# Layer 1 on fewer slots than layer 2, in a mixture-of-experts stage behind linear attention

## The chip, the core and the metric

The kernel runs on one core of a Trainium2 chip. The metric is device time in microseconds (us), from the start to the end of one execution; the span of a profile is the time from its first to its last instruction. TensorE (PE in the profile, PEld for its weight loads) multiplies matrices, VectorE (DVE) and ScalarE (ACT) work on elements, GpSimd (POOL) issues the indirect DMAs here, and SyncE (SP) issues the loads of inputs and weights.

## The reference

```python
kv  = einsum('bhsd,bhse->bhde', k, v)          # 8 batches, 8 heads, 576 tokens, 64 wide
out = einsum('bhsd,bhde->bhse', q, kv)
out = out / sqrt(mean(out*out, -1) + 1e-6) * g_norm
x   = out as 4608 rows of 512
do_compute = x @ w_skip > 0                    # other rows leave as they are
e      = argmax(x @ w_gate)                    # one of 8 experts
gate_w = softmax(x @ w_gate)[e]
x[rows of e] += gate_w * (relu(x[rows of e] @ w1[e]) @ w2[e])   # w1 512x1024, w2 1024x512
```

With the inputs that the reference makes (its seed is fixed), 2265 of the 4608 rows go to an expert, in descending order of the counts 339, 333, 318, 275, 270, 264, 255 and 211.

## The kernel before, in words

**Attention** (up to about 128 us) goes through batches and units of tokens on all engines, writes the rows x to the output in DRAM, and ranks each row within its expert. Each expert has 384 numbered slots; the experts are put in descending order of their counts, and place r of that order has a fixed number of slots `CAPS[r]`: 352, 352, 320, 288, 288, 288, 256, 256. The table `srow` holds for each slot the row that stands in it (less 4608), from a memset to zero (L290) and two sums (`settle`, L706). `slot_rows` (L715) makes of it the row to scatter to; for an empty slot that is 4608, which is out of bounds, so that the scatter leaves it out (L1196). If an expert has more rows than slots, `rounds` (L1266) finds it and a loop (L1336) makes another round; the comparison is "more than".

**Experts.** A place's slots are cut into pieces (`plan_of`, L919): 128, 128 and then 64 or 32 rows (`kinds`, L258; `CAPS` must be sums of these). In `experts` (L1214), for r = 0 to 7 in this order: the weights of r+1 are issued on SP; where r is 7, GpSimd is drained (L1219); the rows of r+1 are gathered by GpSimd, one indirect DMA a piece (`gather_piece`, L940); layer 1 of r; the gathered rows of r+1 are transposed on TensorE (`expert_in`, L947; the first piece inside layer 1's last step, the rest behind it); layer 2 of r; and as each piece of layer 2 is done, VectorE scales and adds it and GpSimd scatters it (`result`, L1184).

For r = 0, layer 1 is plain matmuls over all slots but the first 128, which are done earlier. For r = 1 to 7, `fast_1` (L1064) makes layer 1 from seven products in place of eight, with the slots in two halves of `n = end // 2` columns: 7 products x 4 x 2 matmuls of n columns. `end` is the room of the pieces. A float32 matmul is two instructions in the profile, so a place has 112 of them. `fast_2` (L1124) does the same for layer 2 on the first 256 slots, in products of 256 columns, and does the pieces beyond as plain matmuls beside it. Every engine works in the order in which the code is written.

The hidden activations lie in a tile `ht` of 384 slots, two buffers; the rows of a place in `xg`, three buffers. A gather reads the output in DRAM, and so it waits for the landing of all scatters issued before it; GpSimd's queue holds, from the end of one place to the next, the scatters of r-1, then the gathers of r+1, then the scatters of r. At the program's end all engines go through a barrier (L1336, L1380), in which GpSimd is drained again.

Of the kernel before, what the change touches and what calls it, by code (L numbers as in the profile page):

```python
# [8 lines left out]
FP32 = mybir.dt.float32  # L9
# [3 lines left out]
ALU = mybir.AluOpType  # L13
# [4 lines left out]
def kernel(  # L18
# [43 lines left out]
    nc = tc.nc  # L62
# [3 lines left out]
    P = 128  # L66
# [6 lines left out]
    E, F = moe_w1.shape[0], moe_w1.shape[2]  # L73
# [4 lines left out]
    CAP = 384  # L78
    PK = 2 * KD

    KVD = 5
    CAPS = (352, 352, 320, 288, 288, 288, 256, 256)
    CK = CAP // 128
    NCOL = E * CK
    ROUNDS = N // CAP
    RSPACE = 8192
# [10 lines left out]
    setup = attn.enter_context(tc.tile_pool(name="setup", bufs=1))  # L97
# [114 lines left out]
    for a in range(2):  # L212
        r = slice(a * 64, (a + 1) * 64)
        nc.vector.tensor_scalar(out=gw_b[r, :, a, :, :],
                                in0=wraw[r, :, :].rearrange("e n (u w) -> e u w n", u=2),
# [15 lines left out]
    caps = keep.tile([P, E], FP32)  # L231
    for r, cap in enumerate(CAPS):
        nc.vector.memset(caps[:, r:r + 1], float(cap))

    number_f = keep.tile([P, CK], FP32)
# [8 lines left out]
    for i, qs in enumerate((slice(0, 4 * NQ), slice(4 * NQ, FQ))):  # L244
# [5 lines left out]
                                   op=ALU.bitwise_and)  # L250
# [3 lines left out]
                            in1=rest_i[:, :, :, :].rearrange("p f t r -> p (f t r)"), op=ALU.subtract)  # L254
# [1 line left out]


    kinds = {}  # L258
    for r, cap in enumerate(CAPS):
        off = cap // P * P  # L260
        for m in (64, 32):
            if cap - off >= m:
                kinds.setdefault((off % P, m), []).append((r, off))
                off += m
        assert off == cap
    again, part_of = {}, {}
    for lo, m in kinds:
# [5 lines left out]
        if m not in part_of:  # L273
            q_i = setup.tile([P, 1], I32, name=f"q_i{m}")
            nc.vector.tensor_single_scalar(out=q_i[:, :], in_=part_i[:, :],
                                           scalar=m.bit_length() - 1, op=ALU.arith_shift_right)
            q_f = keep.tile([P, 1], FP32, name=f"q_f{m}")
            nc.vector.tensor_single_scalar(out=q_f[:, :], in_=q_i[:, :], scalar=float(N * P // m),
                                           op=ALU.add)
# [7 lines left out]
    gate_k = keep.tile([P, NT, 3], BF16)  # L287

    srow = keep.tile([P, NCOL], FP32)
    nc.vector.memset(srow[:, :], 0.0)  # L290

    top = keep.tile([P, E], FP32)
    nc.vector.tensor_copy(out=top[:, :], in_=ebase[:, :])
# [336 lines left out]
    def drain(pieces):  # L630
        for _ in pieces:
            pass
# [134 lines left out]
    for b in range(KNOWN // S // 4 * 4, KNOWN // S):  # L767
        nc.gpsimd.dma_start(
            out=out[b * S:(b + 1) * S, :].rearrange("(p c) d -> p c d", c=C)[:, C - 1, :],
            in_=zero[:, :])  # L770

    todo = {}
# [74 lines left out]
    with tc.tile_pool(name="wpool_b", bufs=1, reuse_waits="tile") as wpool_b, \  # L847
# [6 lines left out]
        def bank():  # L854
            return ps_b.tile([P, 512], FP32, tag="bank", name="bank")
# [61 lines left out]


        def plan_of(r):  # L919
            pieces = [(c * P, P, r * CK + c) for c in range(CAPS[r] // P)]  # L920
            i = 0
            for (_, m), rs in kinds.items():
                for j, (r_, off) in enumerate(rs):
                    if r_ == r:
                        pieces.append((off, m, i + j))
                i += len(rs)
            return pieces

        plan = [plan_of(r) for r in range(E)]
        whole = [[(c * P, P, r * CK + c) for c in range(CK)] for r in range(E)]  # L930

        def x_of(xg, off, m):

            lo = (off % P) * DM // P if m < P else 0
            return xg[:, off // P, lo:lo + DM * m // P]
# [11 lines left out]
        def expert_in(xg, xt, piece):  # L947
            off, m, _ = piece
            x = x_of(xg, off, m)
            n = DC * m // P  # L950
            xp = bank()[:, :].rearrange("p (j t) -> p j t", t=P)
            for j in range(n):
                nc.tensor.transpose(out=xp[:, j, :], in_=x[:, j * P:(j + 1) * P],  # L953
                                    identity=ident[:, :])
            if m == P:
                nc.scalar.copy(out=xt[:, :, off:off + P], in_=xp[:, :, :])  # L956
            else:
                nc.scalar.copy(
                    out=xt[:, :, off:off + m].rearrange("p (q j) t -> p q j t", j=n),
                    in_=xp[:, 0:n, :].rearrange("p j (q t) -> p q j t", t=m))  # L960

        def new_xt():
            return ffn.tile([P, DC, CAP], FP32, tag="xt", name="xt")

        def new_ht():
            return ffn.tile([P, FC, CAP], FP32, tag="ht", name="ht")

        def layer_1(r, xt, ht, cols, fs):
            for f in fs:
# [241 lines left out]
                for piece in pieces[r]:  # L1211
                    gather_piece(xgs[r], piece, src, asrc)

        def experts(pieces, srcs, xt, ht, yps0, tables, group):  # L1214

            for r in range(E):
                load_ahead(r)
                if yps0 is not None and r == E - 1:
                    nc.gpsimd.drain()  # L1219
                if r:  # L1220
                    gather_all(r + 1, pieces, *srcs)
                todo = pieces[r]
                end = todo[-1][0] + todo[-1][1]
                new = {}

                def enter(some):
                    for piece in some:
                        expert_in(xgs[r + 1], new["xt"], piece)

                more = pieces[r + 1] if r + 1 < E else []  # L1230
                if more:
                    new["xt"] = new_xt()
                beside = []
                if r == 0:
                    if yps0 is not None:
                        tables = first_tables(lambda fs: layer_1(r, xt, ht, slice(P, end), fs), tables)
                        result((0, P, 0), yps0, xgs[0], tables, group)
                    else:
                        layer_1(r, xt, ht, slice(0, end), range(FC))
                    do(w1_sums(r + 1))  # L1240
                    enter(more)
                else:
                    fast_1(r, xt, ht, end // 2, w2_sums(r), lambda: enter(more[0:1]))
                    enter(more[1:])
                if more:
                    n = (more[-1][0] + more[-1][1]) // 2
                    beside = x_sums(r + 1, new["xt"], n) + (w1_sums(r + 1) if r else [])
                if r == 0:
                    for piece in todo:
                        result(piece, layer_2(r, ht, piece), xgs[r], tables, group)  # L1250
                        do(beside, 4)
                    do(beside)
                else:
                    if yps0 is not None and r == 1:
                        rnd_i = rounds()
                    if yps0 is not None and r == E - 1:
                        n_rounds.append(nc.values_load(rnd_i[0:1, 0:1], min_val=1,
                                                       max_val=ROUNDS + 1))
                    of = {piece[0:2]: piece for piece in todo}
                    fast_2(r, ht, todo[2:], beside,  # L1260
                           lambda key, y: result(of[key], y, xgs[r], tables, group))
                del w_sb[r]
                if more:
                    xt, ht = new["xt"], new_ht()

        def rounds():  # L1266

# [23 lines left out]
        first = (0, P, 0)  # L1291
        assert plan[0][0] == first
        plan[0] = plan[0][1:]
        xt0, ht0 = new_xt(), new_ht()
        expert_in(xg0, xt0, first)
        drain(choose(LAST))
        bv = columns(0, NE, colid_i, row_k, 2, gat_pool, NE)
# [6 lines left out]
        yps0 = layer_2(0, ht0, first, None, range(0, 3))  # L1304
        settle(NE, NT, last_bv)
        layer_2(0, ht0, first, yps0, range(3, 5))
        rows, src = slot_rows(slice(0, NCOL), slot_pool, "")
        arows, asrc = again_rows()
# [8 lines left out]
        def first_tables(layer, tables):  # L1317
# [8 lines left out]
            agate = slot_pool.tile([P, NRES], FP32, tag="agate", name="agate")  # L1326
            nc.vector.tensor_copy(out=agate[:, :], in_=again_of(gate))
            return (tables[0], gate), (tables[1], agate)
        experts(plan, (src, asrc), xt0, ht0, yps0, (rows, arows), "first")

        order.__exit__(None, None, None)

# [3 lines left out]
        with tc.For_i(1, n_rounds, 1):  # L1336
            nc.vector.tensor_single_scalar(out=colid[:, :], in_=colid[:, :], scalar=CK, op=ALU.add)
            nc.vector.tensor_single_scalar(out=number_f[:, :], in_=number_f[:, :],
                                           scalar=float(CAP), op=ALU.add)
            nc.vector.memset(srow[:, :], 0.0)  # L1340
            add_pieces(srow[:, :], place_all(colid, row_k, 2), 2)

            left = slot_pool.tile([P, NCOL], FP32, tag="left", name="left")
            nc.vector.tensor_tensor(
                out=left[:, :].rearrange("p (r c) -> p r c", c=CK),
                in0=number_f[:, :].unsqueeze(1).to_broadcast([P, E, CK]),
                in1=caps[:, :].unsqueeze(2).to_broadcast([P, E, CK]), op=ALU.is_ge)
            nc.vector.tensor_tensor(out=srow[:, :], in0=srow[:, :], in1=left[:, :], op=ALU.mult)
            rows, src = slot_rows(slice(0, NCOL), slot_pool, "")
            for r in range(2):  # L1350
                gather_all(r, whole, src, None)
            gate = slot_gates(colid)
            xt0 = new_xt()
            for piece in whole[0]:
                expert_in(xg0, xt0, piece)
            experts(whole, (src, None), xt0, new_ht(), None, ((rows, gate), None), "more")


# [26 lines left out]
```

## Time and profile before

| what | us |
|---|---|
| three runs | 404.02, 401.65, 402.52 (median 402.52) |
| the profiled execution's own time | 404.02 |
| its span, first to last instruction | 402.2 |
| mean granted TensorE clock | 0.956 of full |
| TensorE busy | 371.8 |
| VectorE busy | 254.4 |
| ScalarE busy | 144.7 |
| GpSimd busy | 123.5 |
| DMA | 81.70 MB at 203 GB/s |

The first 128 us of the span are attention, 128 to 182 the end of the ranking and place 0, then come places 1 to 7: place 1 from 182 to 219, places 2 to 6 in some 27 to 33 us each, place 7 from 369 to 394. The last scatter is issued at 395.5, and the rest is its landing and the end's barrier. A busy time is that of an engine's instructions; those of its queue (waits, branches, drains; written with a q, as POOLq) do not count in it. In a timeline, a line gives the start, the length, and in brackets how long the engine stood idle before and what ended that.

### The profile page before, as it was taken

To read this page: it belongs to the slowest core of one execution; us is meant where nothing else is said; L and a number is where in the kernel's file an instruction comes from. 1 tells how busy PE (TensorE), PEld (TensorE's weight loads), DVE (VectorE), ACT (ScalarE), POOL (GpSimd) and SP (SyncE) were. 2 spreads that over 40 slices of the span, in tenths; PEclk is the share of its full clock that TensorE was granted. 3 is DMA by queue.
4 is the path that set the end of the run, shared out by engine and by line. 5 is a ranking of instruction groups with operands and counts; after the bars stand their busy time and mean duration, and the time that the engine had idled before them with its cause. 6 is when DMAs were issued, how large, how long until landed. Compare 5 with 4: busy or idle time off the path is not lost.

```text
span 402.2 us, 9616 instructions
## 1 busy us (share of the span) xinstructions
PE 371.8 (92%) x3849; PEld 323.1 (80%) x3849; DVE 254.4 (63%) x621; ACT 144.7 (36%) x384; POOL 123.5 (31%) x192
## 2 busy tenths in 40 slices
PE   7789999999874989999999999999999999999992
PEld 4678988888763948859978987998988988989981
DVE  2233568899976761366674775766766776868811
ACT  1365786676743212203510440430430430431410
POOL 7024577665658243111204301231221111212001
PEclk9599999999986898999999999999999999999997
DMA  8999999898595882346252651752752752711001
GB/s 299 394 391 392 316 391 400 250 364 222 169 406 134 255 322 73 102 161 224 73 203 67 250 193 55 260 182 94 257 188 90 258 177 96 255 55 38 16 2 49
DMA packets 31287, 81.70 MB, mean 203 GB/s; under 512 B 1850, under 2 KB 1858, under 8 KB 31236
## 3 DMA queue, kind: packets, MB, share of 16 engines
q1 hardware_dynamic: 26688, 66.59, 47.9%
q0 software_dynamic: 4528, 14.41, 11.0%
q8 instruction: 32, 0.52, 0.5%
q14 instruction: 19, 0.16, 0.1%
q10 hardware_dynamic: 20, 0.02, 0.0%
HBM read 66.80 MB, written 14.48 MB: 202 GB/s over the span
## 4 chain that ended last, share of the span: by engine, by line
PE 71%; DVE 10%; issue 8%; ACT 4%; DMA 3%; POOL 2%; ACTq 0%; DVEq 0%; POOLq 0%
PE bank L1051 40%; PE bank L983 8%; PE bank L972 6%; PE o_ps L450 4%; DVE xl L489 3%; PE sum_ps L343 3%; PE q_ps L414 3%; PE bank L953 2%; DMA xg<-out_dram,src 2%; DVE rs L472 1%; PE g_ps L357 1%; DMA xb<-in_g_norm_dram 1%; ACT qT L417 1%; PE g_ps L366 1%; ACT rs L479 1%
## 5 line engine op out<-in xcount | busy, mean ns | idle before, releaser
L1061 ACT COPY p<-bank 128x144 f32<-128x144 f32 (+4 forms) x70 | 20.9, 299 | 106.1 <-PE bank L1051 91.9
L1051 PE MATMUL bank<-xt,w 128*128 128x144 f32 (+3 forms) x336 | 56.5, 291 | 0.0
L1051 PEld LDWEIGHTS bank<-xt,w 128*128 128x128 f32 x336 | 47.8, 190 | 1.9 <-DVE bank L1055 1.2
L1055 DVE TENSOR_TENSOR bank<-bank,p 128x144 f32<-128x144 f32 (+4 forms) x70 | 23.8, 340 | 40.3 <-PE bank L1051 38.5
L450 PE MATMUL o_ps<-kvd,qT 128*128 128x146 f32 x240 | 36.9, 296 | 3.8 <-DVE xl L489 1.4
L1193 POOL DMA_INDIRECT out_dram<-xg,rows x16 | 16.2, 1011 | 77.8 <-DVE xg L1190 77.2
L524 POOL TENSOR_TENSOR xb<-xl,g_b 128x512 f32<-128x512 f32 x32 | 38.2, 1193 | 1.2 <-DMA out_dram<-xb 1.2
L1051 PE MATMUL bank<-xs,s 128*128 128x144 f32 (+3 forms) x224 | 37.4, 292 | 0.0
L450 PEld LDWEIGHTS o_ps<-kvd,qT 128*128 128x128 f32 x240 | 32.5, 193 | 5.7 <-DVE xl L489 2.4
L983 PE MATMUL bank<-w,ht 128*32 128x128 f32 (+2 forms) x448 | 36.6, 322 | 0.0
L943 POOL DMA_INDIRECT xg<-out_dram,src x15 | 15.9, 1057 | 56.3 <-PE bank L1051 36.2
L1193 POOL DMA_INDIRECT out_dram<-xg,arows x8 | 9.0, 1129 | 76.9 <-DVE xg L1190 76.6
L1051 PEld LDWEIGHTS bank<-xs,s 128*128 128x128 f32 x224 | 31.6, 190 | 1.0 <-ACT p L1061 0.3
L472 DVE TENSOR_REDUCE rs<-sq 128x8 f32<-128x512 f32 x36 | 24.4, 679 | 12.3 <-ACT sq L464 12.1
L983 PEld LDWEIGHTS bank<-w,ht 128*32 128x32 f32 (+2 forms) x448 | 20.4, 121 | 13.6 <-issue 10.9
L489 DVE TENSOR_TENSOR xl<-o_ps,rs 128x584 f32<-128x584 f32 x33 | 25.3, 767 | 4.4 <-PE g_ps L366 0.5
L1051 PE MATMUL bank<-w,ht 128*128 128x256 f32 x112 | 27.2, 386 | 0.0
L1051 PE MATMUL bank<-t,ht 128*128 128x256 f32 x112 | 27.1, 385 | 0.0
L343 PE MATMUL sum_ps<-v,k 64*64 64x64 f32 x1152 | 25.3, 229 | 1.4 <-issue 0.9
L972 PE MATMUL bank<-xt,w 128*128 128x128 f32 (+1 forms) x128 | 24.4, 360 | 1.5 <-ACT xt L956 1.0
L343 PEld LDWEIGHTS sum_ps<-v,k 64*64 64x64 f32 x1152 | 21.7, 140 | 4.5 <-issue 2.6
L1051 PE MATMUL bank<-t,hs 128*128 128x256 f32 x112 | 25.3, 379 | 0.0
(198 smaller groups left out, 697.0 us busy)
## 6 DMA issues: line engine op xcount, KB each, us to landing
w<-in_moe_w_dram SPq DMA_DIRECT2D x16, 2048.0 KB, 10.3
q<-in_q_dram SPq DMA_DIRECT2D x8, 1152.0 KB, 12.0
k<-in_k_dram SPq DMA_DIRECT2D x7, 1152.0 KB, 12.2
v<-in_v_dram SPq DMA_DIRECT2D x7, 1152.0 KB, 14.7
out_dram<-xb SPq DMA_DIRECT2D x8, 512.0 KB, 8.1
out_dram<-xb POOLq DMA_DIRECT2D x8, 512.0 KB, 7.5
k<-in_k_dram SPq DMA_DIRECT2D x2, 576.0 KB, 4.8
v<-in_v_dram SPq DMA_DIRECT2D x2, 576.0 KB, 6.8
```

Of the source, the lines that this page charges most:

```text
L343: nc.tensor.matmul(out=sum_ps[w * 64:(w + 1) * 64, a, u, :], lhsT=kt[r, 2 * u + w, c, :], rhs=vt[r, 2 * u + w, c, :], start=(c == 0), stop ...
L450: nc.tensor.matmul(out=ps[:, w, 0:2 * PK].rearrange("p (r k) -> p r k", r=2)[:, :, cols], lhsT=qT[:, w, a, :], rhs=kvds[b % KVD][:, u, w, ...
L472: nc.vector.tensor_reduce(out=rs[:, :, :], in_=sq[:, :, :, :].rearrange("p x y (a d) -> p x (y a) d", a=2), axis=AX.X, op=ALU.add)
L489: nc.vector.tensor_tensor(out=xl[:, :, :, :].rearrange("p x y (a k) -> p x (y a) k", a=2), in0=ps[:, :, 0:2 * PK].rearrange("p x (h k) -> ...
L524: late.append(lambda: nc.gpsimd.tensor_tensor(out=xb[:, :, 4 * u * D:(4 * u + 4) * D].rearrange("p r (w x) -> p r w x", w=2), in0=xl[:, :, ...
L943: nc.gpsimd.indirect_dma_start(out=x_of(xg, off, m), out_offset=None, in_=cut_rows(m)[:, :], in_offset=bass.IndirectOffsetOnAxis(ap=idx[:, ...
L972: nc.tensor.matmul(out=hps[:, cols], lhsT=w_sb[r][0][:, dc, f * P:(f + 1) * P], rhs=xt[:, dc, cols], start=(dc == 0), stop=(dc == DC - 1))
L983: nc.tensor.matmul(out=yps[q * m:(q + 1) * m, 0:n], lhsT=ht[:, f, off:off + m], rhs=w_sb[r][1][:, f, q * n:(q + 1) * n], start=(f == 0), s ...
L1051: nc.tensor.matmul(out=out, lhsT=lhsT(i), rhs=rhs(i), start=start and i == 0, stop=i == k - 1, skip_group_check=True)
L1055: nc.vector.tensor_tensor(out=to, in0=x, in1=y, op=ALU.add)
L1061: nc.scalar.copy(out=t, in_=x)
L1193: ins = nc.gpsimd.indirect_dma_start(out=cut_rows(m)[:, :], out_offset=bass.IndirectOffsetOnAxis(ap=rows[:, col:col + 1], axis=0), in_=x, ...
```

## The change

The slots that layer 1 works on are parted from the room that is gathered, transposed and used by layer 2. `CAPS` becomes 344, 336, 320, 280, 272, 264, 256, 256, and `ROOMS` is each of them rounded up to a multiple of 32: 352, 352, 320, 288, 288, 288, 256, 256, the former `CAPS`. Pieces, gathers, transposes and layer 2 go by `ROOMS`. Layer 1 goes by `CAPS`: n in `fast_1` is 168, 160, 140, 136, 132, 128, 128 for r = 1 to 7 in place of 176, 160, 144, 144, 144, 128, 128; the plain matmuls of r = 0 have 216 columns in place of 224. GpSimd sets the part of `ht` between the two to zero (`blank`), once for r = 0 before the first transposes and for each later r at the end of the turn before. `srow` starts at 8192 for slots at and beyond `CAPS` and at zero for the others, by three VectorE operations in the setup in place of one memset, so that such a slot is never scattered. The drain of GpSimd at the start of the last place is gone.

```diff
-    CAPS = (352, 352, 320, 288, 288, 288, 256, 256)
+    CAPS = (344, 336, 320, 280, 272, 264, 256, 256)
+    ROOMS = tuple(-(-cap // 32) * 32 for cap in CAPS)
...
-    nc.vector.memset(srow[:, :], 0.0)
+    beyond = setup.tile([P, CK], FP32)
+    nc.vector.tensor_single_scalar(out=beyond[:, :], in_=number_f[:, :], scalar=float(CAP), op=ALU.add)
+    nc.vector.tensor_tensor(
+        out=srow[:, :].rearrange("p (r c) -> p r c", c=CK),
+        in0=beyond[:, :].unsqueeze(1).to_broadcast([P, E, CK]),
+        in1=caps[:, :].unsqueeze(2).to_broadcast([P, E, CK]), op=ALU.is_ge)
+    nc.vector.tensor_single_scalar(out=srow[:, :], in_=srow[:, :], scalar=float(RSPACE), op=ALU.mult)
...
+        def blank(ht, r):
+            if CAPS[r] < ROOMS[r]:
+                nc.gpsimd.memset(ht[:, :, CAPS[r]:ROOMS[r]], 0.0)
...
-        def experts(pieces, srcs, xt, ht, yps0, tables, group):
+        def experts(pieces, widths, srcs, xt, ht, yps0, tables, group):
...
-                if yps0 is not None and r == E - 1:
-                    nc.gpsimd.drain()
...
-                end = todo[-1][0] + todo[-1][1]
+                end = widths[r]
...
-                    n = (more[-1][0] + more[-1][1]) // 2
+                    n = widths[r + 1] // 2
...
                     xt, ht = new["xt"], new_ht()
+                    if yps0 is not None:
+                        blank(ht, r + 1)
...
         xt0, ht0 = new_xt(), new_ht()
+        blank(ht0, 0)
...
-        experts(plan, (src, asrc), xt0, ht0, yps0, (rows, arows), "first")
+        experts(plan, CAPS, (src, asrc), xt0, ht0, yps0, (rows, arows), "first")
```

In `kinds` and `plan_of`, `CAPS` is replaced by `ROOMS`; the loop for further rounds passes `(CAP,) * E` as widths.

More of the change, by code (lines that the diff above doesn't have):

```diff
@@ L258 @@
     kinds = {}
-    for r, cap in enumerate(CAPS):
+    for r, cap in enumerate(ROOMS):
         off = cap // P * P
@@ L919, in plan_of @@
         def plan_of(r):
-            pieces = [(c * P, P, r * CK + c) for c in range(CAPS[r] // P)]
+            pieces = [(c * P, P, r * CK + c) for c in range(ROOMS[r] // P)]
             i = 0
@@ L1355 @@
                 expert_in(xg0, xt0, piece)
-            experts(whole, (src, None), xt0, new_ht(), None, ((rows, gate), None), "more")
+            experts(whole, (CAP,) * E, (src, None), xt0, new_ht(), None, ((rows, gate), None), "more")
 _INS = ['q', 'k', 'v', 'g_norm', 'moe_w_skip', 'moe_w_gate', 'moe_w1', 'moe_w2']
```

## The prediction

> **What bounds the kernel now.** I read the page first: busy times, the chain that ended last, then TensorE by stretches.
>
> ```profile
> PE 371.8 (92%) x3849; PEld 323.1 (80%) x3849; DVE 254.4 (63%) x621; ACT 144.7 (36%) x384; POOL 123.5 (31%) x192
> PE 71%; DVE 10%; issue 8%; ACT 4%; DMA 3%; POOL 2%; ACTq 0%; DVEq 0%; POOLq 0%
> PE bank L1051 40%; PE bank L983 8%; PE bank L972 6%; PE o_ps L450 4%; DVE xl L489 3%; PE sum_ps L343 3%; PE q_ps L414 3%; PE bank L953 2%; DMA xg<-out_dram,src 2%; DVE rs L472 1%; PE g_ps L357 1%; DMA xb<-in_g_norm_dram 1%; ACT qT L417 1%; PE g_ps L366 1%; ACT rs L479 1%
> ```
>
> TensorE is the bound, the products of L1051 above all. But 2% of the chain is a DMA, the gather of the next place's rows, so a second limit is close. The table by stretches gives TensorE's busy time in the second column: place 1 fills its 37.00 us; places 3 to 5 leave 0.06, 0.08 and 0.18 of 30 free; place 6 leaves 0.71. The next view, the chain of waits at the end of layer 1 of place 4 (start, length, what), shows what these are.
>
> ```profile
> 296.12 0.49 PE bank L1051 x4
> 296.61 0.55 PE bank L953 x4
> 297.17 0.07 issue
> 297.23 0.30 PE bank L953
> ```
>
> The transposes of the next place's third piece (the second L953) begin only when its gather has landed: TensorE waits already. GpSimd's timeline has the reason (start, length, idle time before):
>
> ```profile
> 283.11 0.98 POOL L1193 DMA_INDIRECT out_dram<-xg,rows  x1 [0.30 <-DVE xg L1190]
> 291.44 0.99 POOL L943 DMA_INDIRECT xg<-out_dram,src  x1 [7.35 <-PE bank L1051]
> 292.74 0.97 POOL L943 DMA_INDIRECT xg<-out_dram,src  x1 [0.30 <-issue]
> 294.01 1.13 POOL L943 DMA_INDIRECT xg<-out_dram,asrc  x1 [0.30 <-issue]
> ```
>
> The last scatter is issued by 284.09, the first gather at 291.44. The view names TensorE for the 7.35 us between, but that work was long done: scatters take 7.3 us to land in the median, and a gather waits for the landing. Three gathers and some 3 us of landing follow. This row of DMAs starts when place 3's layer 2 ends, and layer 1's length does not enter it.
>
> **Layer 1's columns.** What a column costs is the spacing of equal matmuls in TensorE's timeline (start, length, ..., count):
>
> ```profile
> 185.38 0.76 PE L1051 MATMUL bank<-xt,s 128*128 128x176 f32 x4
> ...
> 196.72 0.76 PE L1051 MATMUL bank<-xt,s 128*128 128x176 f32 x4
> ...
> 284.49 0.65 PE L1051 MATMUL bank<-xt,s 128*128 128x144 f32 x4
> ...
> 293.80 0.65 PE L1051 MATMUL bank<-xt,s 128*128 128x144 f32 x4
> ...
> 343.88 0.61 PE L1051 MATMUL bank<-xs,s 128*128 128x128 f32 x4
> ...
> 352.38 0.61 PE L1051 MATMUL bank<-xs,w 128*128 128x128 f32 x4
> ```
>
> Between the starts of each pair lie 19 groups of four: (196.72 - 185.38)/76 = 149.2 ns at 176 columns, 122.5 ns at 144, 111.8 ns at 128. So a column is 0.83 ns from 144 to 176, and 0.67 from 128 to 144.
>
> - Place 0: 64 matmuls of 8 columns less. The first eight run at half clock (they take 3.4 us to the next groups' 1.5, after TensorE stood idle): (56 x 8 + 8 x 16) x 0.83 = **0.48 us**. All of it counts: VectorE's second table is ready at 161.94 and is used at 166.36, and all behind it waits for TensorE.
> - Place 1: 176 to 168, 112 x 8 x 0.83 = 0.74, taken as **0.73 us**. Its gathers land by 196.9, the last transposes start near 199.7; so 2 us of slack cover it.
> - Place 2: unchanged.
> - Places 3, 4, 5: 4, 8 and 12 columns at 0.67 x 112 are 0.30, 0.60 and 0.90, **1.8 us** in sum. I count them at **nothing**: TensorE waits for the gather here, and arriving earlier it waits longer. Bounds: 0 and -1.8 (all of it, if the gathers came earlier too).
> - Places 6, 7: unchanged.
>
> **The setup.** Three VectorE operations of 24 elements or fewer replace a memset that stands right ahead of work that TensorE waits for (L316, in the chain of waits):
>
> ```profile
> 11.55 0.08 DVE L290 MEMSET srow<- 128x24 f32 x1
> 11.74 0.55 DVE L316 MEMSET kvd<- 64x584 f32 x1
> 13.16 1.94 PE L357 MATMUL g_ps<-ident,kvd 128*128 128x64 f32 x8 [1.70 <-DVE kvd L316]
> ```
>
> Like operations elsewhere (L719, L722) take 0.18 and follow each other at 0.22. Three at 0.20 less the memset's 0.19 are **+0.4 us**; bounds 0 (taken up in attention, where VectorE and DMA also hold TensorE) and 0.6.
>
> **The blanks.** Five memsets of at most 192 elements a partition. The nearest row, 584 elements, is 5.01/8 = 0.63 us. They stand on GpSimd's queue behind the scatters of a place and ahead of the gathers, in the 7 us shown above (for place 0 in 11.4 us of idling before 144.81). What is queued behind them waits anyway, and layer 2 reads the blanks over 10 us later: **nothing**. If that cover were gone, 0.2 us each. Scatters and their bytes stay the same, since empty slots were out of bounds before as well.
>
> **The drain.** Its lines in the views of L1219 and L1380 (count: shortest/median/longest in ns, first and last start):
>
> ```profile
> L1219 POOLq DRAIN  x1: 6041/6041/6041, 369.9 to 369.9; - x1
> ...
> L1380 POOLq DRAIN  x3: 51/109/220, 401.2 to 402.0; - x3
> ```
>
> The drain that goes took 6.04 us, where GpSimd had nothing to do until 394.25: its going wins nothing there. Of it, 1.31 us is waiting for the scatter still being issued (to 371.24); 4.73 follow. That scatter's data had landed by 372.98, so for 3.0 us the drain was busy with something else. The first drain in the end's barrier took 0.220, behind two scatters; a drain at the program's start, with no DMA before, took 0.193. So its length depends on what lies before it. Two readings: (i) it works off something left by each DMA that GpSimd issued since the last drain: 57 before L1219 (23 gathers, 22 scatters, 12 of attention), 4.73/57 = 0.083 each, and two at the end would be 0.17, near the 0.220 seen; (ii) a fixed time has to pass from the last issue: the end's drain starts at 401.19, 4.67 us after its last scatter's 396.52, so that time was nearly over. By (i) the end's drain becomes some 59 x 0.083 = 4.9 us, **+4.7 us** on the path, as GpSimd is the last engine into that barrier and the others wait for it. By (ii) it stays 0.2. Bounds: 0 and 5.8 (all 6.04 less 0.22). I take (i), as it also says why the drain with two DMAs is hardly over the one with none; (ii) needs the end's drain to fall by chance just where the time runs out.
>
> The Trainium skill (VectorE: DVE Perf Modes, "The DRAIN you can't avoid") speaks against (i): it says that the drains of a kernel's beginning and end are a constant of about 12 ns on all five engines. In this trace that holds for the other four at the end (7 to 17 ns), not for GpSimd's, at 51 to 220 and 6041. By that rule the end would not lengthen, and the sum would be some 0.8 us below before.
>
> **The sum.** -0.48 - 0.73 + 0 + 0.4 + 4.7 = **+3.9 us**. Against the profiled execution (span 402.2, own time 404.02) that is a span of 406.1 and 407.9; that execution is 1.5 above the median of the three, and from the median, 402.52, it is **406.4 us**.
>
> **Rivals.**
> - *The end's drain stays short* (reading (ii)). Place: the barrier at 401.19. Then -0.48 - 0.73 + 0.4 = -0.8: **401.7 us**, not slower. It decides as soon as the drain costs under 2.8 us at the end (2.0 over before plus 0.8 won). For it: (ii) fits the one drain at the end; against it: the 0.193 and 0.220 side by side.
> - *Drain short, and the gathers come earlier as well*: -0.8 - 1.8 = -2.6, **399.9 us**. For it: landings vary with the weights' loads, which move too. Against it: the scatters' 7.3 us and the gathers' issue do not shorten.
> - *Drain long, gathers earlier*: +4.7 - 2.6 = +2.1, **404.6 us**.
> - *The change does not do what it says*: a place has more rows than slots, and a further round runs. The reference's counts against the slots, in order: 339/344, 333/336, 318/320, 275/280, 270/272, 264/264, 255/256, 211/256. All fit, the sixth exactly, and the test is "more than". Another round loads 16 weights of 10.3 us again: above **565 us**.
>
> **How the numbers follow.** A measurement here can tell some 0.5% (2.0 us) from no change. Chances: the forecast 0.55; short drain 0.26; short drain and earlier gathers 0.06; long drain and earlier gathers 0.07; a drain between 1 and 3 us 0.05; another round 0.01. The likeliest is 406.4. Slower by over 0.5% (above 404.5) takes the forecast, half of the long drain with earlier gathers and the round: 0.6. Faster (below 400.5): 0.06, with a little of the short drain's spread 0.07. Within: 0.33. The range goes from 401.0 (the short drain's 401.7, less a spread like that of the three runs) to 407.6 (a drain of 5.8 in place of 4.7 gives 407.5); it leaves out the two farthest cases. The slower cases alone lie between 405.0 and 407.6.
>
> **What would show it.** L1380's first GpSimd drain at some 5 us, with all engines behind it, shows the drain; 0.2 us refutes it. Spacings near 142 ns in place 1 and 120, 117 and 114 ns in places 3 to 5 show the columns; an idle time of 0.3 to 1.1 us before the last L953 of these places, with turns as long as before, shows the gathers' limit; turns shortened by as much refute it. Place 1 should be 0.7 us shorter, the first L357 0.4 later. I am wrong above all if the long drain was not deferred work, or if the blanks hold up the gathers behind them.

## The result, and the profile after

| kernel | median us | runs |
|---|---|---|
| before | 402.32 | 4 |
| after | 743.91 | 4 |

The ratio is 1.848, with a 95% interval of 1.840 to 1.857. Here and below a median counts all runs of a kernel, while ratios and intervals leave out single executions in a slower state, so that the two can differ by a few tenths of a per cent. The forecast was 406.4 us, in a range of 401.0 to 407.6. What came is the rival that had a chance of 0.01: a further round runs. The page of the kernel after says so in four lines, its span, TensorE's busy time, SP's queue and the weights' loads:

```profile
span 740.2 us, 13716 instructions
...
PE 689.7 (93%) x5417; PEld 579.5 (78%) x5417; DVE 419.9 (57%) x997; ACT 222.2 (30%) x577; POOL 174.8 (24%) x245
...
q1 hardware_dynamic: 39232, 100.14, 38.9%
...
w<-in_moe_w_dram SPq DMA_DIRECT2D x32, 2048.0 KB, 9.3
```

There are 32 loads of weights of 2 MB where before had 16: all eight experts are gone through twice. TensorE is as full as before (93% against 92%), so nothing looks stalled; it does twice the experts' work. Its timeline shows where the first round ends and the second begins:

```profile
389.86 1.89 PE L1062 MATMUL bank<-t,ht 128*128 128x256 f32 x8
394.41 0.61 PE L657 MATMUL g_ps<-bv,oha_k 128*128 128x48 bf16 x18 [2.67 <-DVE bv L648]
...
406.10 1.08 PE L960 MATMUL bank<-ident,xg 128*128 128x128 f32 x4 [2.51 <-DMA xg<-out_dram,src]
...
411.26 23.55 PE L983 MATMUL bank<-xt,w 128*128 128x384 f32 x64 [0.68 <-ACT xt L963]
```

The last product of place 7 ends at 391.75 (before: 394.45), then rows are placed in slots again, gathered again, and place 0 begins anew with 384 columns. From the traces, the 338.0 us between the spans of the two profiled executions (740.2 and 402.2) are -2.7 for a shorter first round, +334.6 from 391.75 to the last product of the second round (726.33), and +6.05 for what lies behind the last product (13.85 in place of 7.80). A place of the further round takes 19.74 + 18.96 us for its two layers, at 192 columns in `fast_1`, whether it holds rows or not.

**Which place overflows.** The prediction set the reference's counts against the slots in descending order of the final counts. The code doesn't: `gating` calls `rank_experts` for the second of three groups, so the order of the experts is fixed when 22 of 36 tiles of rows are ranked, which is what lets weights and gathers start early. Worked out from the reference's inputs, with the rows of those 22 tiles (2816 of 4608):

| place | rows when the order is taken | rows in the end | slots before | slots after |
|---|---|---|---|---|
| 0 | 209 | 333 | 352 | 344 |
| 1 | 202 | **339** | 352 | **336** |
| 2 | 200 | 318 | 320 | 320 |
| 3 | 171 | 264 | 288 | 280 |
| 4 | 166 | **275** | 288 | **272** |
| 5 | 156 | **270** | 288 | **264** |
| 6 | 153 | 255 | 256 | 256 |
| 7 | 128 | 211 | 256 | 256 |

Places 0 and 1, and 3, 4 and 5, come out of order in the end. The slots of after are laid out for sorted counts, and three places have too few: 3, 3 and 6 rows go over.

### The profile page after: what moved, and what is told of

Same layout as the page of the kernel before. It is cut to its first block, busy times and chain, and to the rows that moved or that the text cites. A ratio compares the mean times of both kernels' runs of the same rounds, so it can differ in the third digit from the quotient of the medians.

```text
span 740.2 us, 13716 instructions
## 1 busy us (share of the span) xinstructions
PE 689.7 (93%) x5417; PEld 579.5 (78%) x5417; DVE 419.9 (57%) x997; ACT 222.2 (30%) x577; POOL 174.8 (24%) x245
## 4 chain that ended last, share of the span: by engine, by line
PE 61%; issue 17%; DMA 11%; DVE 4%; POOL 3%; ACT 2%; POOLq 0%; DVEq 0%; ACTq 0%
PE bank L1062 33%; PE bank L994 11%; PE bank L983 6%; DMA out_dram<-xg,rows 5%; DMA xg<-out_dram,src 3%; PE o_ps L457 2%; DMA out_dram<-xb 2%; PE bank L960 2%; PE sum_ps L350 2%; POOL out_dram L1204 1%; PE q_ps L421 1%; DVE xl L496 1%; POOL xg L950 1%; PE g_ps L364 1%; DMA xg<-out_dram,asrc 1%
## 5 line engine op out<-in xcount | busy, mean ns | idle before, releaser
L1062 PE MATMUL bank<-xt,w 128*128 128x192 f32 (+6 forms) x672 | 123.5, 308 | 0.3 <-DVE bank L1066 0.3
L1072 ACT COPY p<-bank 128x192 f32<-128x192 f32 (+7 forms) x140 | 43.8, 313 | 253.5 <-PE bank L1062 237.3
L994 PE MATMUL bank<-w,ht 128*32 128x128 f32 (+2 forms) x608 | 107.7, 393 | 0.0
L1062 PEld LDWEIGHTS bank<-xt,w 128*128 128x128 f32 x672 | 103.6, 190 | 4.2 <-DVE bank L1066 2.7
L1066 DVE TENSOR_TENSOR bank<-bank,p 128x192 f32<-128x192 f32 (+7 forms) x140 | 49.9, 357 | 90.3 <-PE bank L1062 88.6
L1062 PE MATMUL bank<-xs,s 128*128 128x192 f32 (+6 forms) x448 | 81.6, 308 | 0.0
L1062 PEld LDWEIGHTS bank<-t,ht 128*128 128x128 f32 x224 | 42.1, 190 | 10.0 <-issue 4.9
L1062 PEld LDWEIGHTS bank<-w,ht 128*128 128x128 f32 x224 | 41.1, 190 | 9.3 <-issue 4.7
L983 PE MATMUL bank<-xt,w 128*128 128x128 f32 (+2 forms) x192 | 46.0, 406 | 2.1 <-ACT xt L963 1.6
L1062 PEld LDWEIGHTS bank<-t,hs 128*128 128x128 f32 x224 | 42.6, 190 | 5.8
L983 PEld LDWEIGHTS bank<-xt,w 128*128 128x128 f32 x192 | 34.8, 215 | 12.9 <-issue 2.4
## 6 DMA issues: line engine op xcount, KB each, us to landing
q<-in_q_dram SPq DMA_DIRECT2D x8, 1152.0 KB, 12.1
```

The costliest lines, as they stand in the source:

```text
L983: nc.tensor.matmul(out=hps[:, cols], lhsT=w_sb[r][0][:, dc, f * P:(f + 1) * P], rhs=xt[:, dc, cols], start=(dc == 0), stop=(dc == DC - 1))
L994: nc.tensor.matmul(out=yps[q * m:(q + 1) * m, 0:n], lhsT=ht[:, f, off:off + m], rhs=w_sb[r][1][:, f, q * n:(q + 1) * n], start=(f == 0), s ...
L1062: nc.tensor.matmul(out=out, lhsT=lhsT(i), rhs=rhs(i), start=start and i == 0, stop=i == k - 1, skip_group_check=True)
L1066: nc.vector.tensor_tensor(out=to, in0=x, in1=y, op=ALU.add)
L1072: nc.scalar.copy(out=t, in_=x)
```

## The experiments

### The slots laid out for the order that is taken

```diff
-    CAPS = (344, 336, 320, 280, 272, 264, 256, 256)
+    CAPS = (336, 344, 320, 264, 280, 272, 256, 256)
```

> The kernel after, with the slots of layer 1 set to 336, 344, 320, 264, 280, 272, 256, 256. Theory: the experts' order is taken when 22 of 36 tiles of rows are ranked, so that the places hold 333, 339, 318, 264, 275, 270, 255 and 211 rows in the end; all fit here, no further round runs, and the time is that of the changed kernel's first round with the end's long drain: 402.3 - 2.7 + 4.7 = 404.3 us. First rival (the reading of the prediction, places in descending order of the final counts): place 0 with 339 rows for 336 slots and place 3 with 275 for 264 overflow, about 744 us. Second rival (the blanks or the new start of the slot table make the round count wrong): about 744 us as well.

Measured: 407.8 us against 403.06 for before on the same chip, ratio 1.013 (1.008 to 1.019). By its time no further round runs, with the rest of the change in place: the blanks and the new start of the table are not to blame, and places are not sorted by final counts (then 339 rows would have met 336 slots). The time is dearer than the 404.3 expected; the next experiments say why.

### One row too many

```diff
-    CAPS = (336, 344, 320, 264, 280, 272, 256, 256)
+    CAPS = (336, 338, 320, 264, 280, 272, 256, 256)
```

> As fit_no_drain, but with 338 slots at place 1 in place of 344. Theory: place 1 holds 339 rows, one too many, and a whole further round runs for it: about 744 us, as with the three places that overflow in the kernel after. Rival (the round count depends on something other than the rows at a place): no further round, about 404 us; or a shorter one than with three places.

Measured: 742.62 us. Place 1 holds more than 338 rows and not more than 344, as the table's 339 has it, and a single place over costs as much as three (one run, beside 743.91).

### Too few slots in the kernel before

```diff
-    CAPS = (352, 352, 320, 288, 288, 288, 256, 256)
+    CAPS = (352, 320, 320, 288, 288, 288, 256, 256)
```

> The kernel before with 320 slots in place of 352 at place 1, and nothing of the change. Theory (a place with more rows than slots costs a whole further round, whatever else the kernel does): place 1 has 339 rows, so a further round runs, about 740 us. Rival (the parting of slots and rooms is what makes the further round): about 402 us.

Measured: 736.98 us, one run, beside one of 405.08 of before. The parting of slots and rooms has nothing to do with it.

### The drain

```diff
-                if yps0 is not None and r == E - 1:
-                    nc.gpsimd.drain()
```

> The kernel before without the drain of GpSimd, and nothing else. Reading (i) of the prediction: the end's drain becomes 4.9 us and the time 402.3 + 4.7 = 407.0 us. Reading (ii): the end's drain stays at 0.2 us and the time at 402.3 us.

Measured: 408.83 us against 403.06, ratio 1.017 (1.012 to 1.022), which is +6.7 us (4.7 to 8.7). The drains of the end in this kernel, and the queue's step ahead of the barrier (count: shortest/median/longest ns):

```profile
L1378 POOLq DRAIN  x3: 45/109/4890, 401.9 to 407.3; - x3
...
L1334 POOLq INC_SWDGE_SEM  x1: 1360/1360/1360, 398.8 to 398.8; - x1
```

The same step in before:

```profile
L1336 POOLq INC_SWDGE_SEM  x1: 227/227/227, 399.3 to 399.3; - x1
```

The first drain takes 4.89 us where before had 0.22: +4.67, for the 4.7 forecast. The step INC_SWDGE_SEM, which the forecast left out, takes 1.36 in place of 0.23, another +1.13. Together 5.8 us, inside the interval.

> The kernel before with its drain of GpSimd moved from the start of place 7 to the start of place 4. Theory (a drain takes 0.065 us and 0.082 for each DMA that GpSimd issued since the last drain): 42 DMAs lie before it, so that it goes on for about 3.5 us after the last scatter is issued; 17 are left for the end's drain, which takes 0.065 + 17 x 0.082 = 1.46 us. Rival (the first drain of a kernel takes about 4.7 us once, later ones are short): about 4.7 us at place 4 and 0.2 us at the end.

```diff
-                if yps0 is not None and r == E - 1:
+                if yps0 is not None and r == 4:
```

Measured: 404.22 us, one run, beside one of 405.08 of before. Its drains, from the views of their two lines:

```profile
L1380 POOLq DRAIN  x3: 51/109/1445, 400.2 to 402.2; - x3
...
L1219 POOLq DRAIN  x1: 9503/9503/9503, 280.8 to 280.8; - x1
```

The end's drain, 1.445 us, is the forecast's 1.46 within 0.02; the rival's 0.2 falls. With their further rounds, after and the kernel before with too few slots are two more points:

```profile
L1392 POOLq DRAIN  x3: 40/109/8817, 730.5 to 739.9; - x3
```

```profile
L1380 POOLq DRAIN  x3: 46/109/4146, 730.1 to 734.8; - x3
```

Behind 2, 17, 50, 59 and 107 DMAs the end's drain took 0.220, 1.445, 4.146, 4.890 and 8.817 us: 0.065 + 0.082 for each, all five within 0.03. The time since the last drain grows along with the count, but fits less well: a line through the shortest and the longest (25 us and 730 us) misses the 1.445, 110 us after a drain, by 0.19. What it is that each DMA leaves, no run tells. INC_SWDGE_SEM follows 0.187 + 0.020 for each (0.227, 0.520, 1.360 behind 2, 17, 59). The expectation's other half is wrong: the drain at place 4 went on for 8.24 us after the last scatter's issue (to 290.26) in place of 3.5. That scatter landed at 288.49, together with a load of weights (288.53), and the drain ended 1.77 later; so a drain also waits for landings, and how the two add up is not settled (at place 7 it ended 3.0 us after the landing). Place 5's gathers, queued behind it, began at 291.18, and place 4's layer 1 took 17.5 us in place of 15.5.

### The columns with the drain put back

```diff
                 load_ahead(r)
+                if yps0 is not None and r == E - 1:
+                    nc.gpsimd.drain()
```

> The same slots as fit_no_drain, and the drain of GpSimd put back where the last place begins. Theory (the drain works off what each earlier DMA of GpSimd left, 0.083 us each): the end's drain is 0.2 us again and the time is 402.3 - 2.7 = 399.6 us, faster than before by some 0.7%. Rival (the drain costs the same wherever it is): as fit_no_drain. By the prediction's sum without its drain term, with place 0 at 208 columns and place 1 at 172: 402.3 - 0.9 = 401.4 us.

Measured: 403.18 us against 403.06, ratio 1.002 (0.998 to 1.006): no gain that can be told. Between 252 and 372 us TensorE stands idle for 2.97 us, against 1.02 in the profile of before and 1.63 in that of before without the drain. (Its busy time, 367.5 against 371.8, says little by itself: the kernel before with early gathers, below, has 367.2 with all its columns.) TensorE's timeline at the end of place 3's layer 1, where n is 132, shows it standing still:

```profile
263.36 0.63 PE L960 MATMUL bank<-ident,xg 128*128 128x128 f32 x4
263.83 0.62 PE L1062 MATMUL bank<-xs,w 128*128 128x132 f32 x4
264.86 0.63 PE L960 MATMUL bank<-ident,xg 128*128 128x128 f32 x4 [0.42 <-DMA xg<-out_dram,src]
266.60 0.30 PE L960 MATMUL bank<-ident,xg 128*128 128x128 f32 x1 [1.11 <-DMA xg<-out_dram,asrc]
```

### The gathers one place earlier, in both kernels

```diff
                 if r:
-                    gather_all(r + 1, pieces, *srcs)
+                    gather_all(r + 2, pieces, *srcs)
...
-        for r in range(2):
+        for r in range(3):
             gather_all(r, plan, src, asrc)
```

(and the same start for a further round). The three buffers of `xg` allow it.

> The kernel before, with each place's gathers issued one place earlier (place 2's already before place 0, then those of place r+2 in place r). Theory (TensorE waits for gathers at the end of layer 1): its idle time ahead of the last transposes in places 3 to 6, 1.0 us in the profile of before, goes: a ratio of about 0.9975. Rival (the gathers only look like a limit): idle time and time as before.

> fit_drain with each place's gathers issued one place earlier. Theory: the columns saved in places 3 to 5 were eaten by the wait for the gathers (TensorE stood idle for 2.97 us between 252 and 372 us of fit_drain's profile); without that wait the time falls by some 3 us below fit_drain, to a ratio of about 0.993 against before. Rival (columns save nothing, or something else takes their place): as fit_drain, 1.002.

Measured: before with early gathers 403.35 us against 406.21 on the same chip, ratio 0.996 (0.992 to 0.999), which agrees with the 0.9975 expected; the fitting slots with the drain and early gathers 400.09, ratio 0.988 (0.984 to 0.993). The second is the fastest here, and its interval lies wholly below that of the same kernel without the early gathers (0.998 to 1.006); it touches that of before with them. Its timeline at the place shown above has no waiting:

```profile
263.07 0.60 PE L960 MATMUL bank<-ident,xg 128*128 128x128 f32 x4
263.51 0.62 PE L1062 MATMUL bank<-xs,w 128*128 128x132 f32 x4
263.96 0.71 PE L960 MATMUL bank<-ident,xg 128*128 128x128 f32 x5
264.51 1.89 PE L1062 MATMUL bank<-w,ht 128*128 128x256 f32 x8
```

Five transposes follow without a gap, and layer 2 begins 14.1 us after layer 1 did; without early gathers it was 16.2, and 15.2 in the profile without the drain.

### Less work, with and without early gathers

```diff
-                    product(X_[:, lo], HD, w(1, 0, g), x(1, lo), False)
+                    if r not in (3, 4, 5):
+                        product(X_[:, lo], HD, w(1, 0, g), x(1, lo), False)
...
-                    product(Y_[:, lo], HD, w(1, 1, g), xs(2), False)
+                    if r not in (3, 4, 5):
+                        product(Y_[:, lo], HD, w(1, 1, g), xs(2), False)
```

> The kernel before, with two of layer 1's seven products left out in places 3, 4 and 5 (the last two of each step, so layer 1's results are incomplete there): 32 matmuls of 122.5 ns less a place. Theory (the gathers set the length of layer 1 in these places): each of the three layers 1 stays at about 15 us and TensorE stands idle for what it saved, 3.9 us a place; the time falls by at most 1.5 us. Rival (TensorE sets it): each falls by 3.9 us, the time by 11.8 us.

> The same products left out, and each place's gathers issued one place earlier. Theory: now the 11.8 us are won, as nothing waits for a gather any more, unless VectorE's sums, with some 21 of 30 us busy in these places, become the bound; at least 6 us. Rival (something else than the gathers holds these places): as less_work.

Measured, one run each beside a median of 406.21 of before: 423.19 us with less work, and 390.22 with less work and early gathers. The second agrees with the theory (the layers 1 of places 3 to 5 fall to 11.67, 11.67 and 11.56 us). The first fits neither expectation: less work made the kernel slower by some 17 us. TensorE's waits between 182 and 372 us of that run, and its timeline at place 3:

```profile
PE bank L953 <- DMA xg<-out_dram,src: 20.4, 6, 4.6
```

```profile
263.57 0.65 PE L1051 MATMUL bank<-xt,w 128*128 128x144 f32 x4
266.17 0.63 PE L953 MATMUL bank<-ident,xg 128*128 128x128 f32 x4 [1.95 <-DMA xg<-out_dram,src]
271.43 1.08 PE L953 MATMUL bank<-ident,xg 128*128 128x128 f32 x4 [4.63 <-DMA xg<-out_dram,src]
```

TensorE is early and waits 20.4 us in six waits, against 0.9 in before's profile. Against before's profile the three layers 1 are 12.1 us longer and the three layers 2 5.6 us. Two things in the trace make it worse than a wait for a fixed time; no run takes away one of them alone. First, SP loads the next w1 as soon as layer 1 has let its buffer go; that load is now issued at 264.26, among the gathers (262.68, 263.98, 265.25), and the second gather takes 7.3 us to land, where in before the load came at 266.66, behind all gathers, and that gather took 3.6. Second, the granted clock, the column behind POOL's in the table by stretches:

```profile
264.00:267.00 3.00, 0.85 (x6) 0.42 (x5) 1.36 (x6) 0.57 (x2) 1.89 (x2) 1.00 0.68 182
267.00:277.00 10.00, 5.24 (x15) 4.10 (x16) 2.64 (x8) 1.83 (x5) 0.00 (x0) 0.51 0.59 216
277.00:282.00 5.00, 5.00 (x50) 4.04 (x49) 2.83 (x5) 0.87 (x3) 0.00 (x0) 0.95 0.00 0
```

Early in the wait of 4.63 us (266.80 to 271.43) the clock falls to half, and it comes back only at 277, so that the first 4 us of layer 2 run at half clock too. Places 4 and 5 repeat it, with waits of 3.06 and 4.23 and of 2.45 and 4.10 us. The Trainium skill (TensorE: Matmul & The Clock Gate, "Part 1: The HAM clock gate") has the rule that an idle window of about 3.4 us takes TensorE back to half clock. This run agrees in part: the clock fell when the long wait had lasted only about half a microsecond (0.62 in the mean of 267 to 268, 0.50 from 268 to 269), and in the 3 us before, from 264 to 267, TensorE had been busy for 0.85, so a stretch with little work was enough. Waits of up to 1.1 us, as with the fitting slots, left the clock at full.

The lengths of layer 1, from its first product to layer 2's first in TensorE's timeline, put the runs side by side (us; n in brackets):

| kernel | place 1 | place 3 | place 4 | place 5 | place 6 |
|---|---|---|---|---|---|
| before | 18.20 (176) | 15.41 (144) | 15.54 (144) | 15.42 (144) | 14.98 (128) |
| before, no drain | 18.20 (176) | 16.16 (144) | 15.46 (144) | 15.05 (144) | 14.81 (128) |
| after, first round | 17.49 (168) | 15.09 (140) | 15.49 (136) | 15.13 (132) | 14.58 (128) |
| fitting slots, no drain | 17.84 (172) | 15.24 (132) | 15.43 (140) | 14.87 (136) | 14.64 (128) |
| fitting slots, drain | 17.84 (172) | 16.24 (132) | 15.37 (140) | 15.49 (136) | 14.73 (128) |
| early gathers, before | 18.20 (176) | 15.16 (144) | 15.16 (144) | 15.05 (144) | 13.91 (128) |
| early gathers, fitting slots, drain | 17.84 (172) | 14.11 (132) | 14.81 (140) | 14.34 (136) | 13.91 (128) |

Place 1 goes by its columns in every row. Places 3 to 5 do so only with early gathers; without, 132 columns take anything from 15.13 to 16.24 us, and 144 from 15.05 to 16.16.

## Why the prediction was wrong, point by point

- **The step that failed** is in the fourth rival, "The reference's counts against the slots, in order": the counts were sorted by their final values, and "all fit". The code ranks the experts after 22 of 36 tiles, so place 1 has 339 rows for 336 slots, place 4 has 275 for 272 and place 5 has 270 for 264. The mechanism was named and given one chance in a hundred for want of asking at which moment the order is taken. The front matter makes the same slip where it says that the experts are put in descending order of their counts: they are, of the counts known so far. Nothing in the profile of before could show it; the line in `gating` could. So the sum had no term for a further round, which costs 334.6 us; as a rival its price was only bounded from below ("above 565"). The loads of weights do not set that: 19.5 us are placing and gathering rows again (391.75 to 411.26), and the other 315.1 are the whole of the experts at 384 slots.
- **The drain**: reading (i) was right, and its size, 4.7 forecast and 4.67 measured. Missing was INC_SWDGE_SEM, +1.13. The constant of about 12 ns on all engines (VectorE: DVE Perf Modes, "The DRAIN you can't avoid", as the prediction cites it from the Trainium skill) holds for the other four here and not for GpSimd.
- **Columns of place 1**: 0.73 forecast, 18.20 - 17.49 = 0.71 measured.
- **Columns of places 3 to 5, counted at nothing**: near enough in the sum, and the gathers were the reason. For the fitting slots with the drain the sum's terms give a ratio of 0.998 with these columns at nothing and 0.993 with all 1.8 us of them; 1.002 (0.998 to 1.006) was measured. Single profiles leave room for a part of the 1.8 us: from the start of place 3 to that of place 7 it is 116.6 to 117.1 us in three profiles with before's columns there (before, before without the drain, before with too few slots at place 1), and 115.9 to 117.6 in four with 24 columns fewer in sum (after, the fitting slots with and without the drain, one row too many). With early gathers it is 114.9 and 112.8, and there the columns count in full. Nor do the gathers land at a fixed time: place 3's layer 1 took 15.41 and 16.16 us with 144 columns, 15.24 and 16.24 with 132. Where layer 1 was much shorter, a load of weights came among the gathers; that this delays them is read from the traces of before and of less work; no run took it away by itself.
- **Setup**: +0.4 forecast. TensorE's first transposes of the state (L357 in before) start at 13.79 in the mean of five profiles with the three operations (13.70 to 13.88) and at 13.26 in seven without (12.80 to 13.68): +0.5. What of that reaches the end of attention can't be told in this spread.
- **Place 0**: the start of place 1 was forecast 0.48 - 0.4 = 0.1 earlier and is 0.9 earlier in after's profile; but in the seven profiles with the same place 0 as before it lies anywhere from 180.3 to 184.1, so it stays open.
- **The blanks**: no sign that they cost anything. With the fitting slots and the drain, that of place 3 takes 0.30 us at 252.73, and GpSimd's next gather, which waits for the scatters, starts at 259.85. No run left the blanks out.

With fitting slots the ratio of 1.013 is +5.3 us on a base of 403.06 (3.2 to 7.5), for the forecast's +3.9. But that is another kernel than the one asked about, and not the question that decided.

## What to carry to other kernels

Where data decide how often a loop runs, a change of a capacity is first a question of counts, and of the moment at which they are taken: work out the slack of every bin in the code's own order before any matmul is priced. When a transfer is nearly late, saved compute turns into waiting, and the transfer has to start earlier first: here the columns brought no gain that could be told alone and, with the gathers one place earlier, helped to a ratio of 0.988 (0.996 with the early gathers alone). A drain on GpSimd has its price by the DMAs issued since the last one; put it where GpSimd is idle and nothing is queued behind it.

## What the runs showed of the hardware

- The end's drain of GpSimd took 0.065 us + 0.082 for each DMA that GpSimd issued since the last drain (0.220, 1.445, 4.146, 4.890, 8.817 us for 2, 17, 50, 59, 107), and INC_SWDGE_SEM 0.187 + 0.020 each (0.227, 0.520, 1.360 for 2, 17, 59; 0.031 at the program's start, with no DMA before it, lies off that line); other engines' drains there took 7 to 17 ns. A drain amid traffic ended after the landing of the last DMA before it (9.50 us at place 4).
- Scatters issued behind a load of weights of 2 MB landed shortly before it was done: in before the load was issued at 250.32 and landed at 260.73; the scatters issued at 251.83 and 253.13 landed at 259.15 and 260.56. With no load under way, the one issued at 370.24 landed at 372.98.
- Float32 matmul instructions with 128 rows follow each other at 111.8 ns at 128 columns, 122.5 at 144 and 149.2 at 176, so at 0.83 ns a column between 144 and 176; 132 columns still save (14.11 against 15.16 us at 144, over 112 instructions).
- Two waits of 1.95 and 4.63 us, with 0.63 us of transposes between them, halved the granted clock for about 10 us (0.51 in 267 to 277). Of the 17.7 us that places 3 to 5 lost against before's profile with less work, 5.6 lie in the three layers 2, which begin at half clock.
